# A retention block feeding a two-layer feed-forward block: two blocks of tokens in turns, one weight conversion per step, polynomial in PSUM, v scaled in place of k

## The chip, the cores and the metric

The kernel runs on one core of one Trainium2 chip. The metric is the device time of one execution in microseconds (us), the median over the runs. TensorE does the matrix products and writes to PSUM, eight banks of 128 partitions by 512 float32; VectorE, ScalarE and GpSimd work element by element; SyncE issues the transfers from and to DRAM. Each engine takes its instructions in program order, and semaphores make it wait for the others.

## The reference

A retention layer over 4 batches, 8 heads, 768 positions and head width 64, then a feed-forward block with the activation h - tanh(h) on the 3072 rows of 512 values that it gives:

```python
gamma = 1.0 - 2.0 ** (-5.0 - np.arange(H, dtype=np.float32))
for t in range(S):
    state = gamma[None, :, None, None] * state + np.einsum('bhd,bhe->bhde', k[:, :, t], v[:, :, t])
    y[:, :, t] = scale * np.einsum('bhd,bhde->bhe', q[:, :, t], state)
...
h = x @ w_in                 # (3072, 512) @ (512, 2048)
g = h - np.tanh(h)
return (g @ w_out)           # (3072, 2048) @ (2048, 512)
```

q, k and v come as float32, the two weight matrices as float64, so the kernel also has to turn float64 bits into float32.

## The kernel before

**Retention in chunks.** The 3072 rows are 24 chunks of 128 positions, six to a batch. The decay is put into the inputs: q is multiplied by gamma^t / 8 and k by gamma^-t (tables `gq`, `gk`), both on GpSimd (`scale_chunk`, L180). For each chunk `turn` (L187) transposes k and q on TensorE, four 128 x 128 transposes each into the PSUM tiles kTp and qTp, which ScalarE copies out as kT and qT. `scores` (L199) makes eight products of k and q, one a head, into two PSUM tiles s, and VectorE multiplies them with the causal mask (a, L209). `outputs` (L213) adds up the chunk's output in the PSUM tile y: eight products of the state so far with q (L226, not in a batch's first chunk), and eight of the masked scores with v (L241). Between the two stand the products of k and v for the state (kv, L231: four of 128 x 128, of which the two 64 x 64 blocks on the diagonal are used; not in a batch's last chunk), which VectorE adds to the state (L237). ScalarE copies y into xT (L244), the transposed input of the feed-forward block.

**Weights.** `load_weights` brings tile i of 32 as raw float64 words (512 KB); `convert` (L128) makes float32 of it: two ScalarE operations (low, L145, then head, L146), four on VectorE (L147 to L153), two on GpSimd (L154, L155). Sixteen tiles are of w_in (`w1`), sixteen of w_out (`w2`), in turns of four.

**Feed-forward block.** The rows are taken in six blocks n of 512, and d_ff in 16 tiles m of 128. One step is one pair (n, m): `up` (L255) makes h in four matmuls of 512 columns (each has two rows in the profile, which is why they count eight), `shrink` (L262) computes g, `down` (L281) multiplies g with the tile of w2 into four PSUM tiles o, which collect the sums over all sixteen m. `downs(LAG)` runs `down` two steps behind `up`. The activation takes five ScalarE operations (u = h^2, th = tanh h, q0, q1, large) and six on VectorE: t = (R - u) h, h = h - th (in PSUM), q0 = (q0 + C0) t, q1 = (q1 + A C1) q0, g = q1 u, and where `large` is set the value h - th is copied over g (L278). t, q0, q1 and u lie in SBUF.

**What sets the order.** The program is written out by hand (`manual_schedule`): each engine's queue is the order of the calls. Ahead of the first step stand eight chunks (`AHEAD = 8`), each with one conversion behind it:

```python
    for ci in range(AHEAD):
        scores(ci)
        load_chunk(ci + 2)
        scale_chunk(ci + 1)
        if ci + 1 < AHEAD:
            turn(ci + 1)
        outputs(ci)
        convert(ci)
        load_weights(ci + 2)
```

Then steps 0 to 95 follow in the order of n and m (L319). Steps 0 to 15 carry one chunk each (chunks 8 to 23), and steps 0 to 11 two conversions each, one ahead of `up` and one behind `outputs`. Steps 16 to 95 have neither. All PSUM tiles come from one pool of eight banks (`bank`, L80). The results leave PSUM through VectorE and ScalarE by turns (L289, L291) and go out by transfers.

Of the kernel before, what the change touches and what calls it, by code (L numbers as in the profile page):

```python
# [15 lines left out]
P = 128  # L16
# [15 lines left out]
def kernel(  # L32
# [32 lines left out]
    AHEAD = 8  # L65
# [11 lines left out]
    ps = ctx.enter_context(tc.tile_pool(name="ps", bufs=8, space=bass.MemoryType.PSUM))  # L77
# [10 lines left out]
    nc.sync.dma_start(out=tab, in_=tables)  # L88
# [7 lines left out]
    gk = columns(CPB * H)  # L96
# [31 lines left out]
    def convert(i):  # L128

        if i not in raws:
            return
        dst, _ = weight_ends(i)
        raw = raws.pop(i).rearrange("p (n two) -> p two n", two=2)  # L140
        lo, hi = raw[:, 0], raw[:, 1]
        head = stage.tile([P, TB], U32, tag="head", name=f"head_{i}")
        power = stage.tile([P, TB], U32, tag="power", name=f"power_{i}", bufs=1)
        low = stage.tile([P, TB], F32, tag="low", name=f"low_{i}")
        nc.scalar.activation(low, lo, AF.Copy, scale=2.0 ** -52)  # L145
        nc.scalar.activation(head.bitcast(F32), hi.bitcast(F32), AF.Abs)  # L146
        nc.vector.tensor_scalar(head.bitcast(F32), head.bitcast(F32), HI_MIN, HI_MAX,  # L147
                                op0=ALU.max, op1=ALU.min)
        nc.vector.tensor_scalar(head, head, 3, 0x3FFFFFF8, op0=ALU.logical_shift_left,  # L149
                                op1=ALU.bitwise_and)  # L150
        nc.vector.scalar_tensor_tensor(head, in0=hi, scalar=0xC0000000, in1=head,  # L151
                                       op0=ALU.bitwise_and, op1=ALU.bitwise_or)
        nc.vector.tensor_scalar(power, head, 0xFF800000, None, op0=ALU.bitwise_and)  # L153
        nc.gpsimd.tensor_tensor(low, low, power.bitcast(F32), op=ALU.mult)  # L154
        nc.gpsimd.tensor_tensor(dst, low, head.bitcast(F32), op=ALU.add)  # L155
# [18 lines left out]
    def scale_chunk(ci):  # L174
        if ci >= NCH:
            return
        j = ci % CPB
        kh, qh, _ = loaded[ci]
        for t, g in ((kh, gk), (qh, gq)):
            nc.gpsimd.tensor_tensor(  # L180
                t, t, g[:, ts(j, H)][:, :, None].to_broadcast([P, H, D]), op=ALU.mult
            )

    def pair(t, p):
        return t[:, ds(2 * p, 2)].rearrange("p h d -> p (h d)")

    def turn(ci):  # L187

        kh, qh, _ = loaded[ci]
        turned[ci] = []  # L190
        for nm, t in (("kT", kh), ("qT", qh)):
            tp = bank(f"{nm}p_{ci}")
            for p in range(NP):
                nc.tensor.transpose(tp[:, ts(p, P)], pair(t, p), ident)  # L194
# [4 lines left out]
    def scores(ci):  # L199
        kT, qT = turned[ci]  # L200
        sp = [bank(f"s{i}_{ci}") for i in range(2)]
# [11 lines left out]
    def outputs(ci):  # L213
# [4 lines left out]
        kh, _, vb = loaded.pop(ci)  # L218
# [3 lines left out]
        yT = bank(f"y_{ci}")  # L222
        if before is not None:
            for h in range(H):
                r = ds(D * (h % 2), D)
                nc.tensor.matmul(yT[r, ts(h // 2, P)], before[r, h // 2, r], qT[r, h // 2],  # L226
                                 start=(h // 2 == 0), stop=False, skip_group_check=True)
        if j < CPB - 1:
            kv = bank(f"kv_{ci}")
            for p in range(NP):  # L230
                nc.tensor.matmul(kv[:, ts(p, P)], pair(kh, p), pair(vb, p),  # L231
                                 start=True, stop=True)
            after = mid.tile([P, NP, P], F32, tag="state", name=f"state_{ci}")
            if before is None:
                nc.vector.tensor_copy(after, quarters(kv))
            else:
                nc.vector.tensor_tensor(after, quarters(kv), before, op=ALU.add)  # L237
            state[0] = after
        for h in range(H):
            i, p = h % 2, h // 2  # L240
            nc.tensor.matmul(yT[ds(D * i, D), ts(p, P)], vb[:, h], a[i][:, p],  # L241
# [6 lines left out]
    o_p = {}  # L248

    def work(tag, dtype=F32):  # L250
        return tmp.tile([P, TB], dtype, tag=tag, name=tag)
# [3 lines left out]
    def up(n, m):  # L255
        hp = bank(f"h_{n}_{m}")
# [5 lines left out]
    def shrink(n, m):  # L262
        hp = hps.pop((n, m))
        u, th, q0, q1, large, t = (work(x) for x in ("u", "th", "q0", "q1", "large", "t"))
# [5 lines left out]
        nc.vector.scalar_tensor_tensor(t, in0=u, scalar=R, in1=hp, op0=ALU.subtract,  # L270
                                       op1=ALU.mult, reverse0=True)
        nc.vector.tensor_tensor(hp, hp, th, op=ALU.subtract)  # L272
        nc.vector.scalar_tensor_tensor(q0, in0=q0, scalar=C0, in1=t, op0=ALU.add, op1=ALU.mult)  # L273
        nc.vector.scalar_tensor_tensor(q1, in0=q1, scalar=A * C1, in1=q0, op0=ALU.add,  # L274
                                       op1=ALU.mult)
        g = gp.tile([P, TB], F32, tag="g", name=f"g_{n}_{m}")
        nc.vector.tensor_tensor(g, q1, u, op=ALU.mult)  # L277
        nc.vector.copy_predicated(g, large.bitcast(I32), hp)  # L278
        gT[n, m] = g

    def down(n, m, j):  # L281
        if m == 0:
            o_p[n, j] = bank(f"o_{n}_{j}")
        nc.tensor.matmul(o_p[n, j], gT[n, m][:, ts(j, P)], w2[:, m], start=(m == 0),  # L284
                         stop=(m == NM - 1))
        if m == NM - 1:
            o = op.tile([P, DM], F32, tag="o", name=f"o_{n}_{j}")
            if j % 2:
                nc.vector.tensor_copy(o, o_p[n, j])  # L289
            else:  # L290
                nc.scalar.copy(out=o, in_=o_p[n, j])  # L291
            nc.sync.dma_start(out=out[ds(n * TB + j * P, P)], in_=o)


    for ci in range(2):
        load_chunk(ci)
        load_weights(ci)
    scale_chunk(0)
    turn(0)
    for ci in range(AHEAD):  # L300
        scores(ci)
        load_chunk(ci + 2)
# [3 lines left out]
        outputs(ci)  # L306
        convert(ci)
        load_weights(ci + 2)

    w = AHEAD  # L310
    waiting = []

    def downs(lag):
        while len(waiting) > lag:
            n, m = waiting.pop(0)
            for j in range(BLK):
                down(n, m, j)

    for n in range(NB):  # L319
        for m in range(NM):  # L320
            ci = AHEAD + n * NM + m
            if ci < NCH:
                load_chunk(ci + 2)
                convert(w)
                load_weights(w + 2)
                turn(ci)
            up(n, m)
            if ci < NCH:
                scores(ci)
                scale_chunk(ci + 1)  # L330
            shrink(n, m)
            waiting.append((n, m))
            downs(LAG)
            if ci < NCH:
                outputs(ci)
                convert(w + 1)
                load_weights(w + 3)
                w += 2
    for j in range(BLK):
        for n, m in waiting:  # L340
            down(n, m, j)
# [54 lines left out]
```

## Time and profile before

| what | value |
|---|---|
| median of 3 runs | 885.01 us (884.57 to 886.36) |
| profiled execution | 880.28 us, span 878.5 us |
| TensorE busy | 806.5 us (92% of the span) |
| VectorE busy | 536.7 us (61%) |
| ScalarE busy | 362.9 us (41%) |
| GpSimd busy | 141.3 us (16%), nothing after the first 300 us |
| mean granted TensorE clock | 0.965 of full speed |

The span runs from the first to the last instruction of the profiled execution. Busy shares are means over stretches of very different character, so they are read stretch by stretch. In rows of the profile PE is TensorE, DVE is VectorE, ACT is ScalarE and POOL is GpSimd; L and a number is a line of the kernel; what follows is output<-input by the program's names, then sizes and the count of instructions. What stands in brackets is the idle time before the instruction and what ended it. In the chain of waits the columns are start, duration and what the end of the program was waiting for at that time.

### The profile page before, as it was taken

How to read it: one execution, taken by the hardware profiler on the slowest of the kernel's cores; microseconds unless marked ns; L12 is line 12 of the kernel's file. 1: busy time of each engine (PE TensorE's matmuls, PEld its weight loads, DVE VectorE, ACT ScalarE, POOL GpSimd, SP SyncE). 2: the span in 40 equal slices, each digit the busy share in tenths (PEclk: the TensorE clock that was granted, in tenths of full speed). 3: DMA queues.
4: the chain of work that ended last, by engine and by line, in shares of the span. 5: the costliest groups of instructions: out<-in, count | busy, mean ns of one | idle time of the engine just before them, and what ended most of it. 6: DMA issues, size and time to landing. Idle time of an engine off the chain costs nothing.

```text
span 878.5 us, 8488 instructions
## 1 busy us (share of the span) xinstructions
PE 806.5 (92%) x2976; PEld 404.3 (46%) x2976; DVE 536.7 (61%) x784; ACT 362.9 (41%) x629; POOL 141.3 (16%) x116
## 2 busy tenths in 40 slices
PE   4644789898889999999999999999999999999997
PEld 3533554454545644444444444444444444444443
DVE  2233499989996546555566555655556655566554
ACT  2212354445543434334443344433444334443343
POOL 3242455555655000000000000000000000000000
PEclk9778689999999999999999999999999999999999
DMA  8453656464653001000010000100001000010001
GB/s 190 93 120 74 140 136 147 115 158 107 146 143 73 1 1 48 0 1 0 1 48 0 1 0 1 48 0 1 0 1 48 0 1 0 1 48 0 1 0 48
DMA packets 83130, 42.67 MB, mean 49 GB/s; under 512 B 75792, under 2 KB 75920, under 8 KB 83088
## 3 DMA queue, kind: packets, MB, share of 16 engines
q1 hardware_dynamic: 83088, 42.13, 19.6%
q8 instruction: 23, 0.38, 0.2%
q14 instruction: 19, 0.16, 0.1%
HBM read 35.83 MB, written 6.29 MB: 48 GB/s over the span
## 4 chain that ended last, share of the span: by engine, by line
PE 77%; DVE 13%; POOL 3%; issue 2%; ACT 2%; DMA 1%; SPq 0%; DVEq 0%; POOLq 0%; ACTq 0%
PE h L258 35%; PE o L284 34%; DVE head L151 2%; DVE head L149 2%; PE y L226 2%; PE y L241 2%; DVE q L274 1%; DVE g L277 1%; PE qTp L194 1%; PE kv L231 1%; DVE a L209 1%; DVE q L273 1%; PE kTp L194 1%; POOL low L154 1%; PE s L204 1%
## 5 line engine op out<-in xcount | busy, mean ns | idle before, releaser
L258 PE MATMUL h<-xT,w 128*128 128x512 f32 x768 | 351.3, 601 | 1.5 <-DVE g L278 1.5
L284 PE MATMUL o<-w,g 128*128 128x512 f32 x768 | 346.6, 594 | 1.2 <-DVE g L278 1.2
L258 PEld LDWEIGHTS h<-xT,w 128*128 128x128 f32 x768 | 146.8, 193 | 181.3 <-issue 177.6
L284 PEld LDWEIGHTS o<-w,g 128*128 128x128 f32 x768 | 144.7, 190 | 180.3 <-issue 173.9
L265 ACT ACTIVATE u<-h 128x512 f32<-128x512 f32 x96 | 57.3, 597 | 341.5 <-PE h L258 341.5
L270 DVE SCALAR_TENSOR_TENSOR t<-u,h 128x512 f32<-128x512 f32 x96 | 65.7, 684 | 190.4 <-ACT th L266 190.4
L274 DVE SCALAR_TENSOR_TENSOR q<-q,q 128x512 f32<-128x512 f32 x96 | 74.9, 780 | 10.4 <-DVE q L273 0.5
L277 DVE TENSOR_TENSOR g<-q,u 128x512 f32<-128x512 f32 x96 | 73.8, 768 | 8.0 <-DVE q L274 0.5
L278 DVE COPY_PREDICATED g<-large,h 128x512 f32<-128x512 int32 x96 | 70.3, 732 | 9.9
L273 DVE SCALAR_TENSOR_TENSOR q<-q,t 128x512 f32<-128x512 f32 x96 | 70.5, 734 | 0.0
L267 ACT ACTIVATE q<-u,tab 128x512 f32<-128x512 f32 x96 | 69.3, 722 | 0.0
L268 ACT ACTIVATE q<-u,tab 128x512 f32<-128x512 f32 x96 | 68.9, 718 | 0.0
L269 ACT ACTIVATE large<-u,tab 128x512 f32<-128x512 f32 x96 | 68.7, 716 | 0.0
L272 DVE TENSOR_TENSOR h<-h,th 128x512 f32<-128x512 f32 x96 | 66.5, 692 | 0.0
L194 PE MATMUL kTp<-tab,k 128*128 128x128 f32 x96 | 20.3, 348 | 47.9 <-POOL k L180 47.9
L154 POOL TENSOR_TENSOR low<-low,power 128x512 f32<-128x512 f32 x32 | 41.2, 1287 | 130.3 <-DVE power L153 115.6
L266 ACT ACTIVATE th<-h 128x512 f32<-128x512 f32 x96 | 56.7, 591 | 0.0
L244 ACT COPY xT<-y 128x512 f32<-128x512 f32 x24 | 14.1, 586 | 93.9 <-PE y L241 93.9
L209 DVE TENSOR_TENSOR a<-s,tab 128x512 f32<-128x512 f32 x48 | 30.8, 684 | 31.0 <-PE s L204 31.0
L155 POOL TENSOR_TENSOR w<-low,head 128x512 f32<-128x512 f32 x32 | 41.4, 1292 | 2.5
L194 PEld LDWEIGHTS kTp<-tab,k 128*128 128x128 f32 x96 | 13.0, 172 | 52.6 <-POOL k L180 51.0
L196 ACT COPY kT<-kTp 128x512 f32<-128x512 f32 x24 | 13.9, 581 | 51.7 <-PE kTp L194 51.7
(28 smaller groups left out, 459.8 us busy)
## 6 DMA issues: line engine op xcount, KB each, us to landing
raw<-in_moe_w_in_dram SPq DMA_DIRECT2D x16, 512.0 KB, 4.7
raw<-in_moe_w_out_dram SPq DMA_DIRECT2D x16, 512.0 KB, 3.8
k<-in_k_dram SPq DMA_DIRECT2D x24, 256.0 KB, 4.7
q<-in_q_dram SPq DMA_DIRECT2D x24, 256.0 KB, 5.3
v<-in_v_dram SPq DMA_DIRECT2D x24, 256.0 KB, 5.8
out_dram<-o SPq DMA_DIRECT2D x24, 256.0 KB, 2.0
tab<-in_tables_dram SPq DMA_DIRECT2D x1, 177.5 KB, 2.4
```

What stands on the lines that cost most here:

```text
L258: nc.tensor.matmul(hp, w1[:, c, ts(m, P)], xT[n][:, c], start=(c == 0), stop=(c == NC - 1))
L265: nc.scalar.activation(u, hp, AF.Square)
L267: nc.scalar.activation(q0, u, AF.Square, bias=bias0)
L268: nc.scalar.activation(q1, u, AF.Square, bias=bias1, scale=math.sqrt(A))
L269: nc.scalar.activation(large, u, AF.Relu, bias=bias_m)
L270: nc.vector.scalar_tensor_tensor(t, in0=u, scalar=R, in1=hp, op0=ALU.subtract, op1=ALU.mult, reverse0=True)
L272: nc.vector.tensor_tensor(hp, hp, th, op=ALU.subtract)
L273: nc.vector.scalar_tensor_tensor(q0, in0=q0, scalar=C0, in1=t, op0=ALU.add, op1=ALU.mult)
L274: nc.vector.scalar_tensor_tensor(q1, in0=q1, scalar=A * C1, in1=q0, op0=ALU.add, op1=ALU.mult)
L277: nc.vector.tensor_tensor(g, q1, u, op=ALU.mult)
L278: nc.vector.copy_predicated(g, large.bitcast(I32), hp)
L284: nc.tensor.matmul(o_p[n, j], gT[n, m][:, ts(j, P)], w2[:, m], start=(m == 0), stop=(m == NM - 1))
```

## The change

**Order of the steps.** Blocks 0 and 1 take turns with quarters of d_ff (four tiles m each), written as runs: block 0 quarter 0; block 1 quarters 0 and 1; block 0 quarters 1 and 2; block 1 quarters 2 and 3; block 0 quarter 3. Blocks 2 to 5 go through all of d_ff as before. At the end of each run the sums leave PSUM: the first run of a block is copied to an SBUF tile, a later one is added to that tile on VectorE, and the last goes out. Five chunks stand ahead of step 0, and chunks 5 to 23 are carried by steps 0, 1, 2, every second step from 3 to 25, and 28 to 31. Each step up to 26 converts one tile.

**PSUM** is divided: four banks for o, two for h, two (`t`) for all of a chunk's tiles once the steps have begun.

**Activation.** h - th goes to th in SBUF, and t, q0 and q1 are replaced by h itself in PSUM, worked on in place.

**Retention.** v is scaled by gamma^-t in place of k; kv is eight products of 64 columns with halved output, and the state has half the width.

**Smaller edits.** In `convert` head comes ahead of low on ScalarE; the tables' transfer is issued from ScalarE's queue; in the opening chunks 0 and 1 are loaded ahead of the first weight tile; a chunk's load is issued three ahead, behind `outputs`; `xp` has five buffers, `gp` four, q0 and q1 one each.

The core of the diff:

```diff
-    AHEAD = 8
-    xp = ctx.enter_context(tc.tile_pool(name="xp", bufs=NB))
+    xp = ctx.enter_context(tc.tile_pool(name="xp", bufs=NB - 1))
-    gp = ctx.enter_context(tc.tile_pool(name="gp", bufs=5))
+    gp = ctx.enter_context(tc.tile_pool(name="gp", bufs=4))
-    def bank(name):
-        return ps.tile([P, TB], F32, tag="ps", name=name)
+    def bank(tag, name):
+        return ps.tile([P, TB], F32, tag=tag, name=name, bufs={"o": 4, "h": 2, "t": 2}[tag])
-    nc.sync.dma_start(out=tab, in_=tables)
+    nc.scalar.dma_start(out=tab, in_=tables)
...
+        nc.scalar.activation(head.bitcast(F32), hi.bitcast(F32), AF.Abs)
         nc.scalar.activation(low, lo, AF.Copy, scale=2.0 ** -52)
-        nc.scalar.activation(head.bitcast(F32), hi.bitcast(F32), AF.Abs)
...
-        kh, qh, _ = loaded[ci]
-        for t, g in ((kh, gk), (qh, gq)):
+        _, qh, vh = loaded[ci]
+        for t, g in ((qh, gq), (vh, gv)):
...
-            kv = bank(f"kv_{ci}")
-            for p in range(NP):
-                nc.tensor.matmul(kv[:, ts(p, P)], pair(kh, p), pair(vb, p),
-                                 start=True, stop=True)
-            after = mid.tile([P, NP, P], F32, tag="state", name=f"state_{ci}")
+            kv = bank(tag, f"kv_{ci}").rearrange("p (n d) -> p n d", d=D)[:, :NP]
+            for h in range(H):
+                nc.tensor.matmul(kv[ds(D * (h % 2), D), h // 2], kh[:, h], vh[:, h],
+                                 start=True, stop=True, skip_group_check=True)
+            after = mid.tile([P, NP, D], F32, tag="state", name=f"state_{ci}")
...
-        u, th, q0, q1, large, t = (work(x) for x in ("u", "th", "q0", "q1", "large", "t"))
+        u, th, large = (work(x, 2) for x in ("u", "th", "large"))
+        q0, q1 = (work(x, 1) for x in ("q0", "q1"))
...
-        nc.vector.scalar_tensor_tensor(t, in0=u, scalar=R, in1=hp, op0=ALU.subtract,
+        nc.vector.tensor_tensor(th, hp, th, op=ALU.subtract)
+        nc.vector.scalar_tensor_tensor(hp, in0=u, scalar=R, in1=hp, op0=ALU.subtract,
                                        op1=ALU.mult, reverse0=True)
-        nc.vector.tensor_tensor(hp, hp, th, op=ALU.subtract)
-        nc.vector.scalar_tensor_tensor(q0, in0=q0, scalar=C0, in1=t, op0=ALU.add, op1=ALU.mult)
-        nc.vector.scalar_tensor_tensor(q1, in0=q1, scalar=A * C1, in1=q0, op0=ALU.add,
+        nc.vector.scalar_tensor_tensor(hp, in0=q0, scalar=C0, in1=hp, op0=ALU.add,
+                                       op1=ALU.mult)
+        nc.vector.scalar_tensor_tensor(hp, in0=q1, scalar=A * C1, in1=hp, op0=ALU.add,
                                        op1=ALU.mult)
...
-        nc.vector.tensor_tensor(g, q1, u, op=ALU.mult)
-        nc.vector.copy_predicated(g, large.bitcast(I32), hp)
+        nc.vector.tensor_tensor(g, hp, u, op=ALU.mult)
+        nc.vector.copy_predicated(g, large.bitcast(I32), th)
...
+        if n in sums:
+            o = sums[n][:, j]
+            nc.vector.tensor_tensor(o, o_p[j], o, op=ALU.add)
...
+    Q = NM // 4
+    runs = [[(0, 0)], [(1, 0), (1, 1)], [(0, 1), (0, 2)], [(1, 2), (1, 3)], [(0, 3)]]
+    runs += [[(n, f) for f in range(4)] for n in range(2, NB)]
...
+    AHEAD = BLK + 1
+    when = [0, 1, 2] + list(range(3, 27, 2)) + [28, 29, 30, 31]
+    with_chunk = {s: AHEAD + i for i, s in enumerate(when)}
...
+    for s, (n, m, first, last) in enumerate(steps):
+        ci = with_chunk.get(s)
+        if ci is not None:
+            turn(ci)
+        convert(AHEAD + s)
+        load_weights(AHEAD + s + 2)
+        up(n, m)
+        if ci is not None:
+            scores(ci, "t")
+            scale_chunk(ci + 1)
+        shrink(n, m)
+        waiting.append((n, m, first, last))
+        downs(LAG)
+        if ci is not None:
+            outputs(ci, "t")
+            load_chunk(ci + 3)
```

Three places show how the queues move. The first is GpSimd in the opening, from the second chunk's scaling to the third weight conversion; low and w1 are a conversion's two halves, the other rows scale a chunk's tensors. Before:

```order
L180 TENSOR_TENSOR k_1_99<-k_1_99,tab_87 128x512
L180 TENSOR_TENSOR q_1_101<-q_1_101,tab_87 128x512
L154 TENSOR_TENSOR low_0_179<-low_0_179,power_0_178 128x512
L155 TENSOR_TENSOR w1_89<-low_0_179,head_0_177 128x512
L180 TENSOR_TENSOR k_2_137<-k_2_137,tab_87 128x512
L180 TENSOR_TENSOR q_2_139<-q_2_139,tab_87 128x512
L154 TENSOR_TENSOR low_1_253<-low_1_253,power_1_252 128x512
L155 TENSOR_TENSOR w1_89<-low_1_253,head_1_251 128x512
```

And now the same stretch of GpSimd's queue:

```order
L180 TENSOR_TENSOR q_1_99<-q_1_99,tab_87 128x512
L180 TENSOR_TENSOR v_1_101<-v_1_101,tab_87 128x512
L154 TENSOR_TENSOR low_0_189<-low_0_189,power_0_188 128x512
L155 TENSOR_TENSOR w1_89<-low_0_189,head_0_187 128x512
L180 TENSOR_TENSOR q_2_107<-q_2_107,tab_87 128x512
L180 TENSOR_TENSOR v_2_109<-v_2_109,tab_87 128x512
L154 TENSOR_TENSOR low_1_267<-low_1_267,power_1_266 128x512
L155 TENSOR_TENSOR w1_89<-low_1_267,head_1_265 128x512
```

k is gone from the queue, q stands where k stood, and v follows it; the conversions keep their places between the chunks.

The second is VectorE between the state of one chunk and what follows the next weight conversion; head and power belong to a conversion, a to the masked scores of a chunk. Before, from step 0 to step 1:

```order
L237 TENSOR_TENSOR state_8_767<-kv_8_762,state_7_656 128x512
L147 TENSOR_SCALAR head_9_778<-head_9_778 128x512
L149 TENSOR_SCALAR head_9_778<-head_9_778 128x512
L151 SCALAR_TENSOR_TENSOR head_9_778<-raw_9_678,head_9_778 128x512
L153 TENSOR_SCALAR power_9_779<-head_9_778 128x512
L147 TENSOR_SCALAR head_10_797<-head_10_797 128x512
L149 TENSOR_SCALAR head_10_797<-head_10_797 128x512
L151 SCALAR_TENSOR_TENSOR head_10_797<-raw_10_697,head_10_797 128x512
L153 TENSOR_SCALAR power_10_798<-head_10_797 128x512
L209 TENSOR_TENSOR a0_9_839<-s0_9_829,tab_87 128x512
L209 TENSOR_TENSOR a1_9_841<-s1_9_830,tab_87 128x512
```

And now, from step 3 to the end of step 4, with th, h and g of the activation of a step without a chunk:

```order
L235 TENSOR_TENSOR state_8_876<-kv_8_867,state_7_771 128x256
L147 TENSOR_SCALAR head_9_893<-head_9_893 128x512
L149 TENSOR_SCALAR head_9_893<-head_9_893 128x512
L151 SCALAR_TENSOR_TENSOR head_9_893<-raw_9_705,head_9_893 128x512
L153 TENSOR_SCALAR power_9_894<-head_9_893 128x512
L270 TENSOR_TENSOR th_912<-h_1_0_906,th_912 128x512
L271 SCALAR_TENSOR_TENSOR h_1_0_906<-u_911,h_1_0_906 128x512
L273 SCALAR_TENSOR_TENSOR h_1_0_906<-q0_914,h_1_0_906 128x512
L275 SCALAR_TENSOR_TENSOR h_1_0_906<-q1_915,h_1_0_906 128x512
L278 TENSOR_TENSOR g_1_0_925<-h_1_0_906,u_911 128x512
L279 COPY_PREDICATED g_1_0_925<-large_913,th_912 128x512
```

One conversion of four rows stands where two stood, the activation follows it directly in a step without a chunk, and its three middle rows read and write h.

The third is TensorE from the last product of chunk 9 to the first scores of chunk 10; y and s are chunk tiles, h and o are of the two projections. Before:

```order
L241 MATMUL y_9_863<-a1_9_841,v_9_638 64x128
L194 MATMUL kTp_10_920<-tab_87,k_10_680 128x128 x4
L194 MATMUL qTp_10_927<-tab_87,q_10_682 128x128 x4
L258 MATMUL h_0_2_934<-xT_0_159,w1_89 128x512 x4
L204 MATMUL s0_10_939<-qT_10_932,kT_10_925 128x128
L204 MATMUL s1_10_940<-qT_10_932,kT_10_925 128x128
```

And now:

```order
L239 MATMUL y_9_1006<-a1_9_976,v_9_678 64x128
L257 MATMUL h_1_2_1054<-xT_1_450,w1_89 128x512 x4
L286 MATMUL o_1_0_0_1076<-w2_90,g_1_0_925 128x512
L286 MATMUL o_1_0_1_1078<-w2_90,g_1_0_925 128x512
L286 MATMUL o_1_0_2_1080<-w2_90,g_1_0_925 128x512
L286 MATMUL o_1_0_3_1082<-w2_90,g_1_0_925 128x512
L191 MATMUL kTp_10_1084<-tab_87,k_10_782 128x128 x4
L191 MATMUL qTp_10_1091<-tab_87,q_10_784 128x128 x4
L257 MATMUL h_1_3_1111<-xT_1_450,w1_89 128x512 x4
L202 MATMUL s0_10_1116<-qT_10_1096,kT_10_1089 128x128
L202 MATMUL s1_10_1117<-qT_10_1096,kT_10_1089 128x128
```

A whole step without a chunk, four matmuls of h and four of o, has come between the two chunks.

More of the change, by code (lines that the diff above doesn't have):

```diff
@@ L197, in turn, with scores @@
             turned[ci].append(s)
-    def scores(ci):
+    def scores(ci, tag):
         kT, qT = turned[ci]
-        sp = [bank(f"s{i}_{ci}") for i in range(2)]
+        sp = [bank(tag, f"s{i}_{ci}") for i in range(2)]
         for h in range(H):
@@ L279, in shrink, with down @@
+        nc.vector.copy_predicated(g, large.bitcast(I32), th)
         gT[n, m] = g
[L281 to L287, printed above, removed]
+    def down(n, m, j, first, last):
+        if first:
+            o_p[j] = bank("o", f"o_{n}_{m}_{j}")
+        nc.tensor.matmul(o_p[j], gT[n, m][:, ts(j, P)], w2[:, m], start=first, stop=last)
+        if not last:
+            return
+        done = m == NM - 1
+        if n in sums:
+            o = sums[n][:, j]
+            nc.vector.tensor_tensor(o, o_p[j], o, op=ALU.add)
+        else:
+            if not done:
+                if j == 0:
+                    parts[n] = op.tile([P, BLK, DM], F32, tag="sum", name=f"sum_{n}")
+                o = parts[n][:, j]
+                if j == BLK - 1:
+                    sums[n] = parts[n]
+            else:
+                if j == 0:
+                    parts[n] = op.tile([P, BLK, DM], F32, tag="sum", name=f"sum_{n}")
+                o = parts[n][:, j]
```

81 lines of the change are left out of this document (34 added, 47 removed).

## The prediction

> **What bounds the kernel now.** I read the span by stages first: the busy time of the engines in four stretches, cut where the first projection matmul starts, where the last step with a chunk of retention ends, and where the last up projection ends. The columns are the stretch, its length, the busy us of each engine with the count of instructions, the granted TensorE clock, the DMA share and GB/s.
>
> ```profile
> 0.00:105.40 105.40, 55.70 (x481) 45.40 (x482) 29.42 (x54) 25.62 (x44) 36.06 (x36) 0.79 0.55 121
> 105.40:316.90 211.50, 194.15 (x1201) 112.94 (x1200) 179.84 (x239) 97.25 (x173) 105.26 (x80) 0.96 0.47 110
> 316.90:866.20 549.30, 549.30 (x1280) 243.22 (x1281) 324.06 (x488) 238.84 (x411) 0.00 (x0) 1.00 0.03 10
> 866.20:878.50 12.30, 7.35 (x17) 2.77 (x15) 3.42 (x5) 1.17 (x2) 0.00 (x0) 1.00 0.22 85
> ```
>
> Three regimes. The third stretch is 80 steps in 549.3 us, 6.866 us each, and TensorE is busy for all of it at full clock: nothing but fewer matmuls shortens it. The first stretch is eight chunks with TensorE busy 55.7 of 105.4 us. The second is 16 steps of 13.22 us with VectorE busy 85%. What can be won lies in the first 317 us.
>
> Second, the chain of waits in the opening (start, us, what), from one scaling on GpSimd to the next.
>
> ```profile
> 13.77 1.05 PE y L241 x16
> ...
> 21.40 1.01 POOL k L180
> 22.45 1.11 PE kTp L194 x4
> 23.57 1.00 PE qTp L194 x4
> 24.57 1.75 PE y L226 x16
> 26.32 1.09 PE kv L231 x8
> 27.41 1.05 PE y L241 x16
> 28.48 0.59 ACT xT L244
> 29.06 0.56 ACT low L145
> 29.63 0.55 ACT head L146
> 30.20 0.44 DVE head L147
> ...
> 32.49 1.27 POOL low L154
> 33.84 1.26 POOL w L155
> 35.10 1.01 POOL k L180
> ...
> 105.38 4.78 PE h L258 x8
> ```
>
> It is a ring: 35.10 - 21.40 = 13.70 us a chunk. The next chunk's scaling stands behind a weight conversion on GpSimd, that conversion behind ScalarE's copy of this chunk's output, that copy behind TensorE, and TensorE behind the scaling. No engine is full; the loop's length is the sum.
>
> Third, a chunk step without conversions, in the time line of TensorE (start, us, engine, line, what).
>
> ```profile
> 297.74 1.16 PE L204 MATMUL s<-qT,kT 64*128 64x128 f32 x16
> 298.83 3.70 PE L284 MATMUL o<-w,g 128*128 128x512 f32 x8
> 302.46 1.09 PE L226 MATMUL y<-qT,state 64*64 64x128 f32 x16
> 303.48 1.16 PE L231 MATMUL kv<-v,k 128*128 128x128 f32 x8
> 304.57 1.09 PE L241 MATMUL y<-a,v 128*64 128x128 f32 x16
> 305.59 0.66 PE L194 MATMUL kTp<-tab,k 128*128 128x128 f32 x4
> 306.52 3.60 PE L258 MATMUL h<-xT,w 128*128 128x512 f32 x8
> 310.05 1.16 PE L204 MATMUL s<-qT,kT 64*128 64x128 f32 x16
> ```
>
> From one s to the next 12.31 us, TensorE without a gap: this is what a chunk step costs when TensorE alone sets it. Taken from start to start, s is 1.09, o 3.63, the state part of y 1.02, kv 1.09, the rest of y 1.02, both transposes 0.93. The steps that also convert take longer, and the time line of VectorE and GpSimd says why.
>
> ```profile
> 145.76 0.43 DVE L149 TENSOR_SCALAR head<-head 128x512 uint32<-128x512 uint32 x1
> 147.59 1.31 POOL L154 TENSOR_TENSOR low<-low,power 128x512 f32<-128x512 f32 x1 [4.16 <-DVE power L153]
> 147.82 1.37 DVE L149 TENSOR_SCALAR head<-head 128x512 uint32<-128x512 uint32 x1
> 154.12 1.49 POOL L180 TENSOR_TENSOR k<-k,tab 128x512 f32<-128x512 f32 x1
> 154.82 1.35 DVE L274 SCALAR_TENSOR_TENSOR q<-q,q 128x512 f32<-128x512 f32 x1
> 274.84 1.05 POOL L180 TENSOR_TENSOR k<-k,tab 128x512 f32<-128x512 f32 x1
> 274.88 0.68 DVE L270 SCALAR_TENSOR_TENSOR t<-u,h 128x512 f32<-128x512 f32 x1
> 286.61 1.29 DVE L209 TENSOR_TENSOR a<-s,tab 128x512 f32<-128x512 f32 x2 [4.88 <-PE s L204]
> 287.82 0.68 DVE L270 SCALAR_TENSOR_TENSOR t<-u,h 128x512 f32<-128x512 f32 x1
> 289.80 0.69 DVE L274 SCALAR_TENSOR_TENSOR q<-q,q 128x512 f32<-128x512 f32 x1
> 291.32 0.74 DVE L278 COPY_PREDICATED g<-large,h 128x512 f32<-128x512 int32 x1
> ```
>
> The same L149 takes 0.43 us alone and 1.37 beside a GpSimd multiplication; L274, whose two inputs lie in SBUF, 0.69 alone and 1.35 beside GpSimd. L270 reads one input from PSUM and takes 0.68 beside GpSimd and 0.68 alone. With two conversions a step, the second always meets the GpSimd half of the first, and the polynomial meets the rest.
>
> **The change, part by part.** *Opening.* Only five chunks come before the first step. k is no longer scaled, so its transposes (22.45 to 23.57, 1.12 us) leave the ring: they run while the conversion does. head now stands ahead of low on ScalarE, and VectorE needs head alone: 0.57 us (29.06 to 29.63) leaves too. The scaled v takes k's place on GpSimd behind q; q is what the ring waits for. The new ring is 13.70 - 1.12 - 0.57 = 12.0 us. For the first y, the second chunk's q now lands ahead of 512 KB of weights; that y ended at 14.82, and I take 14.0 (13.3 to 14.8: TensorE and ScalarE work in between stays). Three rings bring the fourth chunk's y to 50.0. From there to the first projection: 35.10 - 28.48 less 0.57 to the scaling of q, 1.05 to the transpose, 1.00 for it: 8.1 us, so 58.1 where it was 105.38. The scaling that this waits for stands ahead of the fifth conversion.
>
> *The first two steps* have no down projection, which comes two steps late. Step 0: h 4.78 (half clock, as in the row at 105.38), s 1.09, then y waits for the two masked score tiles (1.29, under which its state part of 1.02 fits), y 1.02: 8.2. Step 1: 12.31 less o (3.63) and the state part (a batch's first chunk has none), plus 1.3 of the same wait: 9.0. Together 75.3.
>
> *Steps 2 to 31.* 17 carry a chunk: 12 whole (12.31), three that end a batch and lack kv (11.22), two that begin one (11.29); 13 carry none (6.87). 147.7 + 33.7 + 22.6 + 89.3 = 293.3 us, if TensorE stays the bound. Three things bear on that.
>
> VectorE: one conversion is 2.2 us (30.20 to 32.4, just ahead of the row at 32.49), masks and polynomial together 5.45 (286.61 to 292.06), the polynomial alone 4.24. A chunk step and a plain step need 4.4 + 5.45 + 4.24 + 0.7 for the state = 14.8 us, TensorE 12.31 + 6.87 = 19.2. VectorE has 4.4 us to spare in each two steps, so what the polynomial costs in PSUM is hidden; if that cover went, each 0.1 us on its six instructions would cost 0.6 us a step. GpSimd does two conversions and one scaling, 2 x 2.6 + 2.1 = 7.3 of 19.2.
>
> [...]
>
> [...]
>
> kv: eight products of 64 columns for four of 128. Nearest rows: y at 304.57, which has sixteen records 64 wide and takes 1.02, and half of that with half the moving columns; so 0.5 to 1.1, I take 1.0: -0.09 x 14 = -1.3 (to -8).
>
> Two PSUM banks for a chunk's six tiles: where chunks follow in neighbouring steps (2, 3, 29, 30, 31) the next transpose waits for the copy of y, 0.6 us, five times; and at 29 four additions of partial sums (0.69 each) stand ahead of the state on VectorE, some 2 us more. I put 5 us (2 to 12). Behind a plain step the banks have long been free. The twelve extra evacuations lie under an up projection (3.43 us) on engines with room. Weights and chunks are spread over twice the time at 47% DMA share before, so I count no wait for them; tab on ScalarE's queue is worth up to 0.4 us, within the first term.
>
> 293.3 - 1.3 + 5 = 297.0: step 32 at 372.3.
>
> *The rest*: 64 steps of 6.866 = 439.4, to 811.7; the end as now, 12.3: a span of 824.0. The profiled execution took 880.28 us, 1.78 more than its span: 825.8. The median of the runs is 885.01, 4.73 above it, so in those terms 830.5 us, 6% less.
>
>
> **The rivals.** *Chunk steps keep their present pace* (chance 0.11): the waits between engines, not VectorE's load, make 13.22 us a step (211.5 / 16). 17 x 0.9 = 15 more: 846. For it: a chunk's parts still alternate between four engines in one step. Against it: with no conversion the row sequence above has no gap.
>
> *VectorE stays the bound* (0.08): the conversions and the polynomial meet GpSimd as often as now. At +0.94 (L149) on two of a conversion's four instructions and +0.66 (L274) on three of the polynomial's, two steps need 14.8 + 3.8 + 4.0 = 22.6 against 19.2: 3.4 x 13 pairs = 44 more, 874. Against it: one conversion a step has no GpSimd half of another beside it.
>
> *Slower than before* (0.04): the two banks make each chunk's transpose wait for the state, which stands behind the polynomial on VectorE, and the gap drops the clock. The time line has one such place.
>
> ```profile
> 254.48 0.88 PE L194 MATMUL qTp<-tab,q 128*128 128x128 f32 x4 [2.21 <-DVE g L278]
> 255.15 5.09 PE L258 MATMUL h<-xT,w 128*128 128x512 f32 x8
> ```
>
> A wait of 2.21 us, then h takes 5.09 instead of 3.63: 3.7 us. For all 19 chunks 70 us: 830.5 + 70 = 900. It decides from 54.5 / 19 = 2.9 us a chunk on. Against it: most chunk steps follow a plain one, whose 6.87 us need neither bank. [...]
>
> **How the numbers follow.** The forecast has 0.77. Its own bounds: kv -7, the opening -5 (its TensorE parts are at half clock in the rows, and fewer gaps may warm it), bank waits -3 to +7. The range takes in the first rival with a margin: 818 to 850. The third rival, part of the second and odd cases are left out, about 0.2. A measurement of this kernel can tell about 0.2%, 1.8 us (the runs lie between 884.57 and 886.36). Faster 0.96, same 0.01, slower 0.03.
>
> **What would show it.** First h at 58 (55 to 62), rings of 12 us; chunk steps near 12.3 and plain ones near 6.9 up to step 31; step 32 near 372; VectorE about 77% busy in between, and no L149 kin at 1.37. Wrong if h comes after 65, if chunk steps take 13 or more, or if the 64 last steps are not 6.87.

## The result and the profile after

The changed kernel takes 822.08 us (median of 4 runs, 821.72 to 822.91), the kernel before, run beside it, 885.04 (884.57 to 886.36): a ratio of 0.9288, 95% interval 0.9272 to 0.9304. That is 63.0 us less. The forecast was 830.5, range 818 to 850.

The span by stages again, cut at the same places: the first projection matmul, the first up projection after step 31, the last up projection (columns as before: stretch, length, busy us of PE, its weight loads, VectorE, ScalarE, GpSimd, then granted clock, DMA share, GB/s).

```profile
0.00:60.20 60.20, 34.54 (x353) 28.23 (x354) 16.80 (x33) 16.06 (x27) 22.13 (x24) 0.86 0.71 156
60.20:367.40 307.20, 300.30 (x1745) 161.18 (x1744) 223.20 (x368) 157.47 (x274) 108.53 (x93) 1.00 0.37 91
367.40:806.90 439.50, 439.50 (x1026) 194.66 (x1025) 267.22 (x392) 189.76 (x327) 0.00 (x0) 1.00 0.03 10
806.90:819.90 13.00, 7.37 (x17) 2.77 (x15) 3.55 (x6) 1.17 (x2) 0.00 (x0) 1.00 0.21 81
```

The span went from 878.5 to 819.9, 58.6 less. The first projection starts at 60.2 and not at 105.4: 45.2. From there to the start of step 32 it was 211.5 + 16 x 6.866 = 321.4 and is 307.2: 14.2 less, although three more chunks lie in it. The end is 0.7 longer. In the second stretch TensorE is now busy 300.3 of 307.2 us at full clock, and VectorE 73%.

The ring of the opening, in the chain of waits (start, us, what), from the first chunk's output and then from one scaling of q to the next:

```profile
14.08 1.11 PE y L239 x16
...
21.23 1.01 POOL q L180
...
22.29 1.12 PE qTp L191 x4
23.40 1.90 PE y L224 x16
25.31 1.05 PE kv L229 x16
26.36 1.73 PE y L239 x16
28.11 0.59 ACT xT L242
28.70 0.57 ACT head L145
...
31.58 1.27 POOL low L154
...
34.15 1.05 POOL q L180
```

Neither k's transposes nor the copy of low stand in it, as forecast. It takes 34.15 - 21.23 = 12.9 us, where 12.0 was forecast; the next two rings, by the scalings of q at 34.15, 45.87 and 58.52, are 11.7 and 12.7.

A chunk step and the plain step behind it, in the time line of TensorE (start, us, engine, line, what):

```profile
110.10 0.60 PE L191 MATMUL kTp<-tab,k 128*128 128x128 f32 x4
...
119.22 1.09 PE L224 MATMUL y<-qT,state 64*64 64x128 f32 x16
120.24 0.69 PE L229 MATMUL kv<-v,k 128*64 128x64 f32 x16
120.76 1.04 PE L239 MATMUL y<-a,v 128*64 128x128 f32 x16
121.73 3.70 PE L257 MATMUL h<-xT,w 128*128 128x512 f32 x8
125.27 3.60 PE L286 MATMUL o<-w,g 128*128 128x512 f32 x8
128.71 0.60 PE L191 MATMUL kTp<-tab,k 128*128 128x128 f32 x4
```

TensorE has no idle time in front of any row of the pair, those cut out included. The pair takes 128.71 - 110.10 = 18.61 us; from kv to the rest of y it is 120.76 - 120.24 = 0.52 us, where the forecast had 1.0. In VectorE's time line of the same stretch the conversion's L149 is at its short time:

```profile
112.89 0.43 DVE L149 TENSOR_SCALAR head<-head 128x512 uint32<-128x512 uint32 x1
118.29 0.70 DVE L273 SCALAR_TENSOR_TENSOR h<-q,h 128x512 f32<-128x512 f32 x1
119.09 0.70 DVE L275 SCALAR_TENSOR_TENSOR h<-q,h 128x512 f32<-128x512 f32 x1
```

GpSimd scales v from 118.30 to 119.34, beside both polynomial rows, and neither is longer for it (the mean of all 96 of each line is 0.70 too).

In step 0 it is otherwise. The time lines of VectorE and TensorE, in order of time:

```profile
59.88 1.15 DVE L149 TENSOR_SCALAR head<-head 128x512 uint32<-128x512 uint32 x1
62.66 1.37 DVE L149 TENSOR_SCALAR head<-head 128x512 uint32<-128x512 uint32 x1
66.89 1.09 PE L224 MATMUL y<-qT,state 64*64 64x128 f32 x16 [2.09 <-DVE a L207]
```

The last conversion of the opening and the first of the steps follow each other directly, and both meet GpSimd: L149 takes 1.15 and 1.37 us for 0.43. The masks stand behind them, and TensorE waits 2.09 us. The forecast had named an L149 near 1.37 us as a sign against it; from step 1 on there is none.

### The profile page after: what moved, and what is told of

The parts are those of the page before. It is cut to its first block, busy times and chain, and to the rows that moved or that the text cites. A ratio compares the mean times of both kernels' runs of the same rounds, so it can differ in the third digit from the quotient of the medians.

```text
span 819.9 us, 8908 instructions
## 1 busy us (share of the span) xinstructions
PE 781.7 (95%) x3136; PEld 386.8 (47%) x3136; DVE 510.8 (62%) x796; ACT 364.5 (44%) x629; POOL 130.7 (16%) x116
## 4 chain that ended last, share of the span: by engine, by line
PE 92%; DVE 3%; POOL 2%; ACT 1%; issue 1%; DMA 1%; SPq 0%; DVEq 0%; POOLq 0%
PE o L286 40%; PE h L257 40%; PE y L239 3%; PE s L202 3%; PE y L224 3%; PE qTp L191 2%; PE kv L229 2%; PE kTp L191 1%; DVE head L151 1%; POOL q L180 1%; POOL low L154 1%; DMA q<-in_q_dram 1%; DVE head L149 1%; ACT xT L242 1%; POOL w L155 0%
## 5 line engine op out<-in xcount | busy, mean ns | idle before, releaser
L257 PE MATMUL h<-xT,w 128*128 128x512 f32 x768 | 346.6, 594 | 0.0
L257 PEld LDWEIGHTS h<-xT,w 128*128 128x128 f32 x768 | 143.4, 190 | 170.6 <-issue 170.6
L270 DVE TENSOR_TENSOR th<-h,th 128x512 f32<-128x512 f32 x96 | 66.2, 689 | 163.9 <-ACT th L266 163.9
L279 DVE COPY_PREDICATED g<-large,th 128x512 f32<-128x512 int32 x96 | 71.8, 748 | 10.3 <-ACT qT L194 0.5
L273 DVE SCALAR_TENSOR_TENSOR h<-q,h 128x512 f32<-128x512 f32 x96 | 66.9, 697 | 10.4 <-DVE h L271 0.5
L275 DVE SCALAR_TENSOR_TENSOR h<-q,h 128x512 f32<-128x512 f32 x96 | 66.8, 696 | 10.0
L278 DVE TENSOR_TENSOR g<-h,u 128x512 f32<-128x512 f32 x96 | 66.4, 692 | 7.1
L271 DVE SCALAR_TENSOR_TENSOR h<-u,h 128x512 f32<-128x512 f32 x96 | 65.8, 685 | 0.0
L191 PE MATMUL qTp<-tab,q 128*128 128x128 f32 x96 | 17.2, 308 | 21.1 <-POOL q L180 19.0
L202 PEld LDWEIGHTS s<-qT,kT 64*128 64x128 f32 x384 | 24.1, 193 | 16.3 <-issue 15.3
L202 PE MATMUL s<-qT,kT 64*128 64x128 f32 x384 | 28.8, 291 | 0.7 <-ACT qT L194 0.7
```

Of the source, the lines that this page charges most:

```text
L202: nc.tensor.matmul(sp[h % 2][:, ts(h // 2, P)], kT[r, h // 2], qT[r, h // 2], start=True, stop=True)
L257: nc.tensor.matmul(hp, w1[:, c, ts(m, P)], xT[n][:, c], start=(c == 0), stop=(c == NC - 1))
L270: nc.vector.tensor_tensor(th, hp, th, op=ALU.subtract)
L271: nc.vector.scalar_tensor_tensor(hp, in0=u, scalar=R, in1=hp, op0=ALU.subtract, op1=ALU.mult, reverse0=True)
L273: nc.vector.scalar_tensor_tensor(hp, in0=q0, scalar=C0, in1=hp, op0=ALU.add, op1=ALU.mult)
L275: nc.vector.scalar_tensor_tensor(hp, in0=q1, scalar=A * C1, in1=hp, op0=ALU.add, op1=ALU.mult)
```

## The experiments

The theory: three things bring the gain. The opening has fewer and shorter rings; one conversion a step, with the activations of two blocks between, leaves VectorE time to spare, so that TensorE sets the pace; and kv is shorter. The polynomial's place in PSUM then counts for little, since VectorE has spare time either way. The chief rival (port): it is the polynomial in PSUM, where GpSimd doesn't hold it up (L273 and L275 above, 0.70 beside it), that takes VectorE off the bound. Ratios are to the kernel before, run beside each (884.2 to 884.5), and "more" or "less" is against 822.08 unless said otherwise.

**1. The polynomial back in SBUF**, all else as changed (q0, q1 and t have one buffer each, so that it fits):

```diff
-        q0, q1 = (work(x, 1) for x in ("q0", "q1"))
+        q0, q1, t = (work(x, 1) for x in ("q0", "q1", "t"))
...
-        nc.vector.scalar_tensor_tensor(hp, in0=q0, scalar=C0, in1=hp, op0=ALU.add,
-                                       op1=ALU.mult)
...
+        nc.vector.scalar_tensor_tensor(q0, in0=q0, scalar=C0, in1=t, op0=ALU.add, op1=ALU.mult)
```

> The changed kernel with the old activation: t, q0 and q1 in SBUF, h - th in PSUM. Theory (spread): VectorE has spare time in every pair of steps, so a polynomial that meets GpSimd costs nothing at the end: 822 within 2 us, the three instructions with two SBUF inputs longer on average (0.73 to 0.78 us), chunk and plain step still 18.6 us together. Rival (port): the move into PSUM is what took VectorE off the path; then each pair of steps grows by 1 to 3 us, 835 to 862 us.

823.14 us (822.73 to 823.86), 0.9309 [0.9296, 0.9323]: 1.1 more, and its interval overlaps with that of the changed kernel. In VectorE's time line the long row beside GpSimd is back (GpSimd scales v from 118.89 on, 1.49 us), and then VectorE waits all the same:

```profile
119.58 1.34 DVE L274 SCALAR_TENSOR_TENSOR q<-q,q 128x512 f32<-128x512 f32 x1
...
127.19 0.69 DVE L270 SCALAR_TENSOR_TENSOR t<-u,h 128x512 f32<-128x512 f32 x1 [1.16 <-ACT th L266]
```

The longer row is absorbed: 1.16 us of idle time are left behind it, and the pair of steps still takes 129.31 - 110.70 = 18.61 us. The three instructions with two SBUF inputs came to 0.74, 0.81 and 0.71 us on average, where 0.73 to 0.78 was expected. The rival falls for this kernel.

**2. The kernel before with the polynomial in PSUM**, that alone, the activation written as the change writes it.

> The kernel before with the new activation alone. Over the 96 tiles L273, L274 and L277 stood (44 + 90 + 78) ns above 690 ns, 20 us of VectorE in all, nearly all of it in steps 0 to 11. If VectorE's load sets the pace of those steps, about 20 us go: 863 to 868 us. If waits between engines set it, nothing goes: 885 us.

870.97 (869.48 to 872.29), 0.9849 [0.9831, 0.9867]: 13.6 less than before, where about 20 was expected. So the same edit is worth 13.6 where VectorE is the bound and about 1 where it is not. In the sixteen steps with chunks VectorE's busy time fell by 18.8 us (180.1 to 161.3), near the expected 20, but the steps became only 14.3 shorter (211.65 to 197.35), as VectorE idles 4.5 us more. About half of that (2.5 us before, 4.9 here) is a wait for ScalarE; its longest, in VectorE's time line:

```profile
147.21 0.43 DVE L147 TENSOR_SCALAR head<-head 128x512 f32<-128x512 f32 x1 [2.08 <-ACT head L146]
...
149.72 1.38 DVE L149 TENSOR_SCALAR head<-head 128x512 uint32<-128x512 uint32 x1
```

VectorE now waits 2.08 us for ScalarE's copy of the head, and L149 still meets GpSimd with two conversions a step. Where the rest of the idle time comes from stays open.

**3. k scaled and not v**, with k ahead of q on GpSimd as it was:

```diff
-        _, qh, vh = loaded[ci]
-        for t, g in ((qh, gq), (vh, gv)):
+        kh, qh, _ = loaded[ci]
+        for t, g in ((kh, gv), (qh, gq)):
```

> The changed kernel with k scaled instead of v, k first. Theory (ring): the transposes of k return into the ring of the opening, 1.1 us in each of three to four rings, and in the steps nothing changes: 825 to 827 us. Rival (the ring is set elsewhere, by a transfer or by ScalarE): 822 us.

826.72 (826.50 to 826.94), 0.9349 [0.9335, 0.9363]: 4.6 more, as expected. The first projection starts at 64.8 and not at 60.1: the whole difference lies in the opening.

**4. kv in four products of 128 columns**, and the state 128 wide:

```diff
...
-            for h in range(H):
-                nc.tensor.matmul(kv[ds(D * (h % 2), D), h // 2], kh[:, h], vh[:, h],
-                                 start=True, stop=True, skip_group_check=True)
...
+            for p in range(NP):
+                nc.tensor.matmul(kv[:, p], pair(kh, p), pair(vh, p), start=True, stop=True)
...
```

> The changed kernel with kv as four products of 128 columns and the full-width state. The profile after shows kv at 0.51 us where it was 1.09. If that is what made steps 2 to 31 shorter than forecast, 14 chunks give back 0.58 us each and the opening one or two more: 830 to 832 us. If the price that the prediction took (1.0 us) were the right one: 823 to 824 us.

832.68 (832.40 to 834.09), 0.9420 [0.9403, 0.9438]: 10.6 more. The time line of TensorE has kv back at its old length:

```profile
124.28 1.16 PE L232 MATMUL kv<-v,k 128*128 128x128 f32 x8
125.37 1.09 PE L241 MATMUL y<-a,v 128*64 128x128 f32 x16
```

1.09 for 0.52 us, and the pair 19.23 us for 18.61. Over 14 chunks in steps 2 to 31 that is 8.7 us, and the first projection comes 2.3 us later (62.4), with the longer kv in the rings: 11.0, near the 10.6 measured.

**5. Blocks in plain order, two conversions a step**; five chunks ahead and the chunks spread as changed:

```diff
-    runs = [[(0, 0)], [(1, 0), (1, 1)], [(0, 1), (0, 2)], [(1, 2), (1, 3)], [(0, 3)]]
-    runs += [[(n, f) for f in range(4)] for n in range(2, NB)]
+    runs = [[(n, f) for f in range(4)] for n in range(NB)]
...
-        convert(AHEAD + s)
-        load_weights(AHEAD + s + 2)
+        convert(AHEAD + 2 * s)
+        load_weights(AHEAD + 2 * s + 2)
...
+        convert(AHEAD + 2 * s + 1)
+        load_weights(AHEAD + 2 * s + 3)
```

> The changed kernel with blocks in plain order and two conversions a step (steps 0 to 13); the chunks stay spread. Theory (spread of the conversions): a chunk step needs 2 x 2.2 + 5.45 + 0.4 us of VectorE and about 1.9 more where the second conversion meets GpSimd, a plain step 10.5 us, against 11.8 and 6.87 of TensorE; five pairs lose 4 us each: 840 to 848 us, and the 1.37 us L149 returns. Rival (the spread of the chunks alone does it, taking turns is worth nothing): 822 to 825 us.

845.60 (844.67 to 846.34), 0.9560 [0.9543, 0.9577]: 23.5 more, the largest of the parts. The first projection starts at 60.5, so all of it lies in the steps. The time lines of GpSimd, VectorE and TensorE, in this order:

```profile
124.41 1.32 POOL L154 TENSOR_TENSOR low<-low,power 128x512 f32<-128x512 f32 x1 [3.79 <-DVE power L153]
```

```profile
124.63 1.37 DVE L149 TENSOR_SCALAR head<-head 128x512 uint32<-128x512 uint32 x1
126.04 1.64 DVE L151 SCALAR_TENSOR_TENSOR head<-raw,head 128x512 uint32<-128x512 uint32 x1
...
128.12 1.28 DVE L207 TENSOR_TENSOR a<-s,tab 128x512 f32<-128x512 f32 x2
```

```profile
128.86 1.09 PE L224 MATMUL y<-qT,state 64*64 64x128 f32 x16 [2.27 <-DVE a L207]
```

The second conversion meets the GpSimd half of the first, loses 0.94 us on L149 (1.37 for 0.43) and 0.95 on L151 (1.64 for 0.69), the masks stand behind it, and TensorE waits 2.27 us for them. This is the mechanism that the forecast read from the trace of before, and it is here although the polynomial lies in PSUM. Three pairs of steps, from the projection of a plain step at 110.4 to that of another at 175.7, take 21.8 each for 18.61; 27 conversions in twos last 13.5 steps or 7 pairs: 22 us. The projection of step 14, just behind the last of them, starts at 220.4 for 194.7. The run undoes the single conversions and the turns of the two blocks together, since the turns are what makes one conversion a step enough; it doesn't part them.

**6. The kernel before with five chunks ahead**, that alone (`AHEAD = 8` becomes `AHEAD = 5`).

> The kernel before with five chunks ahead of the first step instead of eight, nothing else. Theory (ring): three rings of 13.7 us leave the opening (-41), three chunk steps of 13.2 us replace plain ones of 6.87 (+19): 860 to 866 us. Rival (a chunk costs the same in the opening and in a step): 885 us.

864.66 (862.97 to 865.22), 0.9773 [0.9755, 0.9791]: 19.5 less than the kernel before beside it, as expected. The first projection starts 35 us earlier (70.3; 41 was expected), and the three chunks cost some 15 us again in the steps (19 was expected): both parts were smaller, and their errors cancel.

**7. GpSimd scales two chunks ahead**, so that the scaling no longer stands behind the conversion that this chunk's output sets off:

```diff
     scale_chunk(0)
+    scale_chunk(1)
...
-        scale_chunk(ci + 1)
+        scale_chunk(ci + 2)
```

> The changed kernel with GpSimd scaling two chunks ahead, so that the next chunk's scaling no longer stands behind a conversion. Theory (ring): the ring of 12 to 13 us opens; what is late next is the masks behind the conversion on VectorE and the loads (1.28 MB a chunk, about 6.5 us at 200 GB/s), 7 to 9 us a chunk: 802 to 812 us, first h at 42 to 50 us. Rival (the ring is not what sets the opening): 820 to 823 us.

804.11 (804.02 to 804.50), 0.9092 [0.9078, 0.9106]: 18.0 less, and the first projection starts 18.0 us earlier, at 42.1. What the rings lose passes in full to the end. The chain of waits has a shorter ring, without GpSimd:

```profile
19.66 1.10 PE y L239 x14
...
20.78 0.59 ACT xT L242
21.36 0.58 ACT head L145
...
22.49 1.16 DVE head L149
...
24.90 1.21 DVE a L207 x2
...
26.15 1.10 PE y L239 x14
```

6.5 us a chunk: this chunk's output, the conversion's VectorE half, the next chunk's masks behind it. This is the fastest of all kernels here, with run 9 level, and faster than both that were compared.

**8. Four chunks ahead**, the fifth moved to step 3:

```diff
-    AHEAD = BLK + 1
-    when = [0, 1, 2] + list(range(3, 27, 2)) + [28, 29, 30, 31]
+    AHEAD = BLK
+    when = [0, 1, 2, 3] + list(range(4, 27, 2)) + [28, 29, 30, 31]
```

> The changed kernel with four chunks ahead of the first step and the fifth to eighth carried by steps 0 to 3. Theory (ring): one ring of 12.3 us goes, one plain step becomes a chunk step (+4.9): 814 to 817 us. Rival (the first steps then wait for the fourth chunk and the conversions, and give it back): 820 to 824 us.

815.71 (815.43 to 819.34), 0.9235 [0.9207, 0.9263]: 6.4 less. The first projection starts at 47.3, 12.8 us earlier: a whole ring is gone. The moved chunk's work comes back in a step, and TensorE waits 2.35 us for the fourth weight tile of the first projection.

**9. Both, 7 and 8.**

> Scaling two chunks ahead and four chunks ahead of the first step, together. With scaling two ahead the opening's ring measured 6.5 us a chunk; one ring less is -6.5, one plain step that becomes a chunk step +4.9: 801 to 804 us, against 804.1 with five. If the gains of the two added up as if they were independent (-18.0 and -6.4): 797.7 us.

804.30 (804.00 to 806.99), 0.9098 [0.9085, 0.9112]: no better than 7 alone, where the two gains added would give 797.7. The time line of TensorE shows how the wait of run 8 has grown (this profiled execution took 806.99, the longest of the five):

```profile
35.04 2.74 PE L257 MATMUL h<-xT,w 128*128 128x512 f32 x6
41.23 1.12 PE L257 MATMUL h<-xT,w 128*128 128x512 f32 x2 [3.45 <-POOL w L155]
42.28 1.98 PE L202 MATMUL s<-qT,kT 64*128 64x128 f32 x16
```

The first projection takes four weight tiles; the fourth is still being converted, TensorE waits 3.45 us for it, and the scores behind the wait take 1.98 us for 1.16.

**10. As 9, with each conversion behind the next chunk's masks**, to shorten the ring of 6.5 us:

```diff
         scale_chunk(ci + 2)
+        if ci:
+            convert(ci - 1)
+            load_weights(ci + 1)
...
-        convert(ci)
-        load_weights(ci + 2)
+    convert(AHEAD - 1)
+    load_weights(AHEAD + 1)
```

> As the one before, and in the opening each conversion is issued behind the next chunk's scores, so that VectorE masks the scores first. Theory (the ring is now ScalarE's copy, the conversion on VectorE, the masks, y): the 2.8 us of conversion leave the ring, TensorE's 4.6 us of work a chunk or the loads (1.28 MB a chunk) set the pace: 795 to 801 us. Rival (loads at 200 GB/s already set 6.5 us): no change against the one before.

807.14 (805.88 to 808.60), 0.9128 [0.9114, 0.9142]: a miss, 2.8 more than 9, though single runs of the two overlap. The rings did shrink, to 4.0 to 5.5 us, and the projection starts at 29.3; but the conversions now come later, and the projection waits three times for them, in TensorE's time line:

```profile
31.87 1.12 PE L257 MATMUL h<-xT,w 128*128 128x512 f32 x2 [1.58 <-POOL w L155]
37.31 2.08 PE L257 MATMUL h<-xT,w 128*128 128x512 f32 x2 [4.31 <-POOL w L155]
40.41 2.08 PE L257 MATMUL h<-xT,w 128*128 128x512 f32 x2 [1.03 <-POOL w L155]
```

Four converted weight tiles, and not the chunks, are the next bound of the opening.

**11. low ahead of head on ScalarE**, the two lines of the conversion exchanged.

> The changed kernel with low ahead of head on ScalarE, as before the change. Theory (ring): 0.57 us in each of three to four rings, nothing in the steps: 823.5 to 825 us. Rival: 822 us.

825.75 (825.43 to 826.41), 0.9339 [0.9326, 0.9351]: 3.7 more. In the chain of waits low stands in each ring again, for 0.57 to 0.68 us, and chunk 5's q is scaled at 61.10 and not at 58.52, 2.6 us later. That this is near four times 0.57 is partly chance: the three rings take 12.9, 13.4 and 13.5 us for 12.9, 11.7 and 12.7, since TensorE's parts differ too: in the second ring kv and the rest of y take 1.12 and 1.70 us for 0.71 and 1.04. The further 1.1 us come in step 0: TensorE waits 2.37 us for the masks, where the changed kernel waits 2.09, and here the rows behind the wait are longer (the rest of y 1.59 for 1.09, k's transposes 1.11 for 0.66, the next projection 3.89 for 3.60). The next step's scores start 3.8 us later (77.87 for 74.08).

**12. The chunks in steps 0 to 18, one in each**, and not in every second step (xp gets a sixth buffer, for the block that is done earlier):

```diff
-    when = [0, 1, 2] + list(range(3, 27, 2)) + [28, 29, 30, 31]
+    when = list(range(NCH - AHEAD))
```

> The changed kernel with chunks 5 to 23 in steps 0 to 18, one a step, instead of every second step; still one conversion a step (xp with six buffers). Theory (spread of the conversions): VectorE needs 2.2 + 5.45 + 0.4 = 8.1 us of a chunk step's 11.8, so TensorE stays the bound, and only the copy of y out of the two shared banks shows, 0.2 to 0.8 us in some twelve steps more: 824 to 832 us. Rival (the spread of the chunks is what took VectorE off the path): 840 us or more.

827.75 (826.88 to 829.37), 0.9362 [0.9349, 0.9376]: 5.7 more. In TensorE's time line a chunk step follows a chunk step:

```profile
127.14 1.05 PE L239 MATMUL y<-a,v 128*64 128x128 f32 x16
128.87 0.66 PE L191 MATMUL kTp<-tab,k 128*128 128x128 f32 x4 [0.69 <-ACT xT L242]
```

The transpose waits 0.69 us for the copy of y here, behind a batch's last chunk, near the 0.6 that the forecast took for neighbouring chunk steps. Behind most chunks the wait is 0.19 us, and a chunk step takes 12.08 us (the projections at 93.20 and 105.28) for 11.74. The changed kernel has twelve fewer such neighbours; 5.7 us over twelve is 0.5 each, of which 0.8 us in all had come by step 2 (its projection at 81.13 for 80.29). From step 2 on TensorE waits for ScalarE's copies alone and never for the masks, so VectorE kept up even so; the plain step between two chunks mainly covers the wait for y.

## Why the prediction was right

**The mechanism held, point by point.** The opening loses k's transposes and low from its ring (runs 3 and 11: 4.6 and 3.7 us) and three of its rings. One conversion a step, with the turns that allow it, ends the meeting with GpSimd from step 1 on (run 5: 23.5), so TensorE sets the pace from step 2 to step 31. Of the rivals, chunk steps at 13.2 us are out: a chunk step is 18.61 less a plain one of 6.87, 11.74. VectorE is no bound (73% busy in the stretch; the forecast had 77% for a pair of steps). Nor does a gap at each chunk's transpose drop the clock: the second stretch runs at 1.00. The polynomial's move into PSUM, for which the sum has no term, cost none in these rows: L273 and L275 take 0.70 us with an input and the output in PSUM, against 0.69 for the kernel before's L274 in SBUF without GpSimd beside it.

**Where sizes were off.** The forecast is 8.4 us above the median.

- *The opening*: the first y ended at 15.2 and not at 14.0, and the three rings took 37.3 us for 36.0, as both parts of y took longer in the first ring than in the rows they came from (1.90 and 1.73 for 1.75 and 1.05). The first projection came 2.0 later than forecast; it ran at full clock (granted 1.00; 3.60 us for 4.78), but the waits behind it were longer, and step 2 began at 78.4 for 75.3: +3.1. The forecast had put the state part of y under step 0's wait for the masks; it began only behind them (66.89, in the rows above), as the two banks of a chunk's tiles still held the scores, and the masks came late behind two lengthened conversions.
- *kv* is the term that was mis-sized. I bounded it by 0.5 and 1.1 and took 1.0, by the nearness of one row; half of y's sixteen records was the right end. 0.52 gives 14 x 0.48 = 6.7 us less. Run 4, which puts the old form back, has 8.3 us more from the projection of step 2 to that of step 32 (295.4 for 287.1).
- *Steps 2 to 31* took 289.0 for 297.0: kv's 6.7, and 1.3 us that are left, chiefly because the bank waits were smaller: TensorE is idle for 2.8 us in these steps, where the sum had 5. The waits are there where chunks neighbour each other, as the time line of TensorE shows at the first of these places, and nowhere else:

```profile
78.40 0.66 PE L191 MATMUL kTp<-tab,k 128*128 128x128 f32 x4 [0.69 <-ACT xT L242]
79.83 0.41 PE L191 MATMUL qTp<-tab,q 128*128 128x128 f32 x2 [0.77 <-ACT kT L194]
```

- *The 64 last steps* took 439.5 for 439.4, the end 13.0 for 12.3. Span: 819.9 for 824.0. That the span is nearer than its parts is luck: +3.1 and +0.8 stand against -8.0.
- *From the profiled execution to the median*: I carried the 4.73 us over by which before's profiled execution lay below its median. The changed kernel's took 821.85, 0.2 below its median: that step failed, and it is 4.5 of the 8.4 us. The runs show where part of it may come from. Runs 2 and 6 have the opening of the kernel before up to the fifth chunk; in their traces the first y ends at 17.06 and 17.86, in before's at 14.82, and run 2's first projection starts 3.3 us later than before's (108.48 for 105.17, in TensorE's time lines). So the execution that the forecast took its opening from had an early start. There is no second trace of the kernel before, so that this makes up the 4.73 is not shown.

**The parts don't add up.** Undone one at a time they cost 23.5 (turns and single conversions), 10.6 (kv), 5.7 (spread), 4.6 (k), 3.7 (low) and 1.1 (polynomial), 49 together; five chunks ahead gave 19.5 on the kernel before. What a part is worth depends on what bounds the stage: the polynomial 13.6 on the kernel before, 1.1 here.

## What to carry to other kernels

Where no engine is full, write down the loop of waits and ask which member need not stand in it: scaling one chunk earlier, a reordering of two calls, took 6 us out of each ring and was worth 18.0 us, more than most edits of the arithmetic. Before an instruction is made cheaper, look whether its engine is the bound in that stage with the other edits made: the same edit was worth 13.6 us and 1.1 us. When two gains are to be added, look for the next thing that comes late: here two gains of 18.0 and 6.4 gave 18.

## What the runs showed of the hardware that was not expected

- A product with 64 moving columns took half of one with 128: sixteen records of kv 0.52 us, sixteen of y 1.02, each from start to start of the rows. So a pair of heads as two 64 x 64 blocks took half the time of one 128 x 128 block of which half is thrown away (run 4: 1.09 us).
- The last instruction of the polynomial, a COPY_PREDICATED with its values in SBUF, was twice as long beside GpSimd in one place. In run 5, in VectorE's time line:

```profile
222.03 1.55 DVE L279 COPY_PREDICATED g<-large,th 128x512 f32<-128x512 int32 x1
```

GpSimd scales q and then v in this time; 0.75 is the instruction's median from 60 to 330 us of this run. In the changed kernel it hardly meets GpSimd: its mean is 0.748, its longest 1.24.
- How long TensorE had waited does not alone tell whether it was slower behind the wait. In the kernel before, the projection took 5.40 and 5.09 us behind waits of 2.20 and 2.21 us (at 172.12 and 255.15, with a granted clock of 0.68 and 0.71 over it), and 3.70 at a granted clock of 1.00 behind one of 2.27 (at 201.03). In run 5 the row behind a wait of 2.27 us kept its short time (y 1.09), in run 8 the scores did so behind 2.35 (s 1.16), and in run 11 the rest of y and k's transposes didn't behind 2.37 (1.59 for 1.09, 1.11 for 0.66). Behind waits of 3.45 and 4.31 us rows took 1.7 and 1.9 times as long (runs 9 and 10: s 1.98 for 1.16, h 2.08 for 1.12). What else decides it is not shown.
